# Batch 2's q and k casts and transposes moved ahead within batch 1, the output weights and batch 3's loads behind them

## Chip, cores and metric

The kernel runs on one core of one Trainium2 chip. The metric is the time of one execution on the device in microseconds (us), the median of several runs. Lower is better.

## What is computed

Sliding-window attention with a linear position bias for 8 batches of 8 heads, 576 tokens and 64 channels, and behind it a two-layer block on the 4608 x 512 result:

```
scores = q k^T / 8, for 0 <= i - j < 128, plus -slope_h * (i - j); elsewhere -1e9
attn   = softmax(scores);  x = attn v, as (4608, 512)
h      = x w_in            # w_in 512 x 2048
g      = h * clip(h + 3, 0, 6) / 6
out    = g w_out           # w_out 2048 x 512
```

Inputs and output are float32; the products run in bf16.

## The kernel before, in words

*Two streams of work on PE.* Attention is done by pairs of heads: 4 pairs per batch, so pair g belongs to batch g // 4, and there are 32 pairs. The two-layer block is done in 9 tiles of 512 tokens, cut into units: an up unit (`moe_up`, L299 on) makes 128 of the 2048 hidden channels with four 128x512 products (L303), an activation on ACT (L307) and a multiply on DVE (L308); a down unit (`moe_down`) adds four products (L320) to the output of 128 tokens. `fill(n)` puts the next n units between the steps of attention. It stops early where an up unit needs tokens of a batch whose attention isn't through.

*The order is written out by hand.* All five engines run under a manual schedule, so each engine executes its instructions in the order of the code. `first_batch` does batch 0; `segment` (L413) does the pairs 4 to 31, and in its step g: `scores(g)`, the exponentials of pair g, `values` of pair g-1 in two parts, `back(g-1)`, and then `stage_next(g)` (L359), which prepares later batches. Between these stand the fills.

*How a pair gets its q and k.* For batches 0 and 1 q and k are loaded as runs of six tokens and transposed on PE (L191). From batch 2 on, q, k and v are loaded by tokens (`load_tokens`, L105: five DMAs of 128 tokens each on SP's queue), cast by GpSimd from float32 to bf16 (`cast_tokens`, L153), and q and k are then transposed by one DMA each on SP's queue (`xbar`, L167) out of the one buffer `tbuf` into `qTb` or `kTb`. So q must have left `tbuf` before k is cast into it, and so on. v is cast into `vbuf` (L157, L160). There are four load buffers, `ldbuf`, given out by `slot_of` (L87).

*What else GpSimd does.* For every pair it applies the window mask: two selects on `pd` (L226), two on `po` (L242) and one on `p4buf` (L246), each after an exponential of ACT; `values` reads their results. It also issues the loads of the weights, which cast to bf16 on the way: `w_in` early and `w_out` (L144, four DMAs) in `load_weights_out`.

*The order around the change.* Before `segment`, SP's queue is given v of batch 1 and q and k of batch 2. Then `stage_next` puts in, always behind the selects of the pair: in pair 4, the cast of batch 1's v; in pair 5, cast and transpose of batch 2's q, then the load of batch 3's q; in pair 6, cast and transpose of batch 2's k, the load of batch 2's v, the issue of `w_out`, the load of batch 3's k; in pair 7, the cast of batch 2's v, the load of batch 3's v, the cast of batch 3's q; in pair 8, the transpose of batch 3's q and the cast of its k. In the text, q2 stands for batch 2's q, and so on.

Of the kernel before, what the change touches and what calls it, by code (L numbers as in the profile page):

```python
# [18 lines left out]
def kernel(  # L19
# [10 lines left out]
    B, H, S, D = q.shape  # L30
# [5 lines left out]
    NP = H // 2  # L36
# [50 lines left out]
    def slot_of(b, nm):  # L87
        if nm != "v" and b < 2:
            return 2 * b
        if b < 2:  # L90
            return 1 - b
        return (1, 3, 2, 0)[(3 * (b - 2) + "qkv".index(nm)) % 4]
# [6 lines left out]
    def load_runs(b, hs):  # L99
        for nm in "qk":  # L100
            nc.gpsimd.dma_start(
                out=ld[b, nm][:, hs, :],
                in_=src_of[nm][b, hs, :, :].rearrange("h (p t) d -> p h (t d)", t=RT))

    def load_tokens(b, nm):  # L105
        t = ldbuf[slot_of(b, nm)][:, 0:NQ * H * D].rearrange("p (j h d) -> p j h d", j=NQ, h=H)
        ld[b, nm] = t
        for j in range(NQ):
            n = min(128, S - j * 128)
            nc.sync.dma_start(out=t[:n, j, :, :],  # L110
                              in_=src_of[nm][b, :, ds(j * 128, n), :].rearrange("h p d -> p h d"))
# [24 lines left out]
    def load_weights_in(lo, hi):  # L136
        for g in range(lo, hi):
            nc.gpsimd.dma_start(
                out=w_in_sb[:, :, ts(g, 512)],
                in_=moe_w_in[:, ts(g, 512)].rearrange("(k p) f -> p k f", p=128))  # L140

    def load_weights_out():
        for g in range(4):
            nc.gpsimd.dma_start(  # L144
                out=w_out_sb[:, ts(g, 4), :],
                in_=moe_w_out[ds(g * 512, 512), :].rearrange("(m p) d -> p m d", p=128))
# [6 lines left out]
    def cast_tokens(b, nm):  # L153
        s = ld[b, nm]
        if nm == "v":
            for lo in (0, 2):
                nc.gpsimd.tensor_copy(  # L157
                    out=vbuf[b % 2][:, lo:lo + 2, :, 0:D].rearrange("p j h d -> p (j h) d"),
                    in_=s[:, lo:lo + 2, :, :].rearrange("p j h d -> p (j h) d"))
            nc.gpsimd.tensor_copy(out=vbuf[b % 2][:LAST, 4, :, 0:D], in_=s[:LAST, 4, :, :])  # L160
            return
        for j in range(NQ):
            m = min(128, S - j * 128)
            nc.gpsimd.tensor_copy(out=tbuf[:m, :, j, :],  # L164
                                  in_=s[:m, j, :, :].rearrange("p (i e) d -> p i (e d)", e=2))

    def xbar(b, nm):  # L167
        dst = (qTb if nm == "q" else kTb)[b % 2]
        nc.sync.dma_start_transpose(out=dst.rearrange("p h j c -> p (h j) c"),
                                    in_=tbuf.rearrange("p h j c -> p (h j c)"))  # L170
# [188 lines left out]
    def stage_next(g):  # L359
        b, hp = divmod(g, NP)  # L360
        if g == 0:
            load_runs(1, slice(0, H))
        if g == 1:
            load_weights_in(2, 4)
        if b == 1:
            if hp == 0:
                cast_tokens(1, "v")
            if hp == 1:
                cast_tokens(2, "q")
                xbar(2, "q")  # L370
            if hp == 2:
                cast_tokens(2, "k")
                xbar(2, "k")
                load_tokens(2, "v")
                load_weights_out()
            if hp == 3:
                cast_tokens(2, "v")
        if b >= 2 and b + 1 < B:
            if hp < 2:
                xbar(b + 1, "qk"[hp])  # L380
            if hp in (0, 2):
                cast_tokens(b + 1, "kkv"[hp])
        if b >= 1 and b + 2 < B:
            if hp > 0:
                load_tokens(b + 2, "qkv"[hp - 1])
            if hp == 3:
                cast_tokens(b + 2, "q")

    def first_batch():
        transposes(0)  # L390
        prepare(1)
        for g in range(NP + 1):
            if g < NP:
                scores(g)
                exp_diag(g, 0)
                exp_diag(g, 1)
            if g + 1 < NP:
                transposes(g + 1)
            if g < NP:
                exp_off(g, 0)  # L400
                exp_off(g, 1)
            if g > 0:
                values(g - 1, (0, 1, 2))
                values(g - 1, (3, 4))
            if g + 2 < NP:
                prepare(g + 2)
            if g > 0:
                back(g - 1)
                done[0] = g
            if g < NP:  # L410
                stage_next(g)

    def segment(lo, hi, fills):  # L413
        for g in range(lo, hi + 1):
# [32 lines left out]
            if g < hi:  # L447
                stage_next(g)
# [55 lines left out]
```

## Time and profile before

| | |
|---|---|
| median of 5 runs | 381.54 us (379.33 to 381.95) |
| the profiled execution's own time | 383.75 us |
| its span, first to last instruction | 382.0 us |
| PE busy | 322.5 us (84%) |
| ACT, DVE, GpSimd busy | 200.4, 172.5, 151.9 us |
| DMA | 51.64 MB, mean 135 GB/s |
| mean granted clock of PE | 0.955 |

PE is the matrix engine, ACT the scalar engine, DVE the vector engine, POOL is GpSimd and SP the engine that issues most DMAs; SPq and POOLq are instructions that issue DMAs. A row of a timeline gives the start in us from the span's start, the duration, the engine, the line of the code, the operation with what it writes and reads, and in brackets how long the engine was idle before it and what it waited for. The queue q1 carries the DMAs that SP issues, q0 those of GpSimd. The granted clock is TensorE's, as a share of full speed. A busy share of the DMA view can exceed 100%, since packets overlap.

### The profile page before, as it was taken

To read this page: it belongs to the slowest core of one execution; us is meant where nothing else is said; L and a number is where in the kernel's file an instruction comes from. 1 tells how busy PE (TensorE), PEld (TensorE's weight loads), DVE (VectorE), ACT (ScalarE), POOL (GpSimd) and SP (SyncE) were. 2 spreads that over 40 slices of the span, in tenths; PEclk is the share of its full clock that TensorE was granted. 3 is DMA by queue.
4 is the path that set the end of the run, shared out by engine and by line. 5 is a ranking of instruction groups with operands and counts; after the bars stand their busy time and mean duration, and the time that the engine had idled before them with its cause. 6 is when DMAs were issued, how large, how long until landed. Compare 5 with 4: busy or idle time off the path is not lost.

```text
span 382.0 us, 6536 instructions
## 1 busy us (share of the span) xinstructions
PE 322.5 (84%) x2445; PEld 162.3 (42%) x2445; DVE 172.5 (45%) x357; ACT 200.4 (52%) x365; POOL 151.9 (40%) x265
## 2 busy tenths in 40 slices
PE   1566877418778979988999999999999999999986
PEld 0454443213333435543555554445455444444432
DVE  5565565304535224543445454544555444344320
ACT  1643666415646346654666776657676443443401
POOL 8751385506366526735562666282334000000000
PEclk9999988856989989998999999999999999999999
DMA  9999909999979959994999699652112110010012
GB/s 170 196 208 182 203 10 185 148 208 198 200 143 218 182 129 157 221 212 118 198 211 243 141 218 222 150 116 72 47 45 47 44 53 31 27 51 33 27 57 82
DMA packets 153135, 51.64 MB, mean 135 GB/s; under 512 B 141200, under 2 KB 148624, under 8 KB 153104
## 3 DMA queue, kind: packets, MB, share of 16 engines
q1 hardware_dynamic: 145504, 44.54, 60.8%
q0 software_dynamic: 7456, 6.55, 10.8%
q8 instruction: 19, 0.31, 0.4%
q14 instruction: 12, 0.10, 0.1%
q10 hardware_dynamic: 144, 0.13, 0.1%
HBM read 36.70 MB, written 9.44 MB: 121 GB/s over the span
## 4 chain that ended last, share of the span: by engine, by line
PE 60%; ACT 8%; DVE 7%; DMA 7%; issue 6%; POOL 6%; SPq 5%; POOLq 0%
PE ops L320 27%; PE hps L303 25%; DMA xT<-avs 4%; ACT r L307 3%; SPq L110 3%; DVE g L308 2%; PE scd L203 2%; DMA ldbuf<-in_v_dram 2%; POOL tbuf L164 2%; POOL pd L226 2%; ACT pd L223 2%; PE av L266 2%; PE tp L191 2%; DMA ldbuf<-in_k_dram 1%; DVE avs L272 1%
## 5 line engine op out<-in xcount | busy, mean ns | idle before, releaser
L308 DVE SCALAR_TENSOR_TENSOR g<-r,hps 128x512 bf16<-128x512 f32 x144 | 99.0, 687 | 147.5 <-ACT r L307 147.4
L307 ACT ACTIVATE r<-hps,bias 128x512 f32<-128x512 f32 x144 | 99.6, 692 | 120.3 <-PE hps L303 119.0
L303 PE MATMUL hps<-xT,w_in_sb 128*128 128x512 bf16 x576 | 153.6, 391 | 8.6 <-DMA xT<-avs 5.6
L320 PE MATMUL ops<-w_out_sb,g 128*128 128x512 bf16 x576 | 147.5, 384 | 4.7 <-DVE osb L334 3.9
L320 PEld LDWEIGHTS <-g 128*128 128x128 bf16 x576 | 56.0, 98 | 79.6 <-issue 16.2
L303 PEld LDWEIGHTS <-w_in_sb 128*128 128x128 bf16 x576 | 53.1, 100 | 59.6 <-issue 11.0
L226 POOL TENSOR_SCALAR_AFFINE_SELECT pd<-pd 128x512 bf16<-128x512 bf16 x64 | 39.3, 633 | 64.3 <-ACT pd L223 62.6
L164 POOL CAST tbuf<-ldbuf 128x512 bf16<-128x512 f32 (+1 forms) x60 | 34.2, 615 | 36.1 <-issue 29.5
L223 ACT ACTIVATE pd<-scd,bias_d 128x512 bf16<-128x512 f32 x64 | 41.1, 684 | 13.3 <-PE scd L203 13.3
L233 ACT ACTIVATE po<-sco,bias_o 128x512 bf16<-128x512 f32 x64 | 44.3, 693 | 0.0
L242 POOL TENSOR_SCALAR_AFFINE_SELECT po<-po 128x512 bf16<-128x512 bf16 x56 | 35.4, 636 | 21.5 <-ACT po L233 19.2
L272 DVE TENSOR_TENSOR avs<-av,rc 128x384 bf16<-128x384 f32 (+1 forms) x60 | 29.7, 495 | 2.1
L263 PE MATMUL av<-vbuf,po 128*128 128x65 bf16 x240 | 24.7, 201 | 5.4 <-DVE avs L272 3.6
L266 PE MATMUL av<-vbuf,pd 128*128 128x65 bf16 x248 | 25.4, 204 | 2.0 <-POOL pd L226 2.0
L266 PEld LDWEIGHTS <-pd 128*128 128x128 bf16 x256 | 21.3, 105 | 12.6 <-POOL pd L226 3.2
L263 PEld LDWEIGHTS <-po 128*128 128x128 bf16 x256 | 21.0, 105 | 10.9 <-DVE avs L272 5.7
L203 PE MATMUL scd<-qTb,kTb 64*128 64x128 bf16 x256 | 14.4, 240 | 12.5 <-DMA kTb<-tbuf 10.8
L157 POOL CAST vbuf<-ldbuf 128x1024 bf16<-128x1024 f32 x16 | 16.3, 1040 | 17.2 <-DMA ldbuf<-in_v_dram 17.2
L271 DVE RECIPROCAL rc<-av 128x6 f32<-128x6 f32 (+1 forms) x60 | 11.0, 184 | 25.9 <-PE av L266 25.9
L236 ACT ACTIVATE p4buf<-sco,bias_d 128x64 bf16<-128x64 f32 x64 | 21.0, 328 | 0.0
L332 ACT COPY osb<-ops 128x512 f32<-128x512 f32 x18 | 10.5, 586 | 19.3 <-PE ops L320 19.3
L203 PEld LDWEIGHTS <-kTb 64*128 64x128 bf16 x256 | 8.2, 102 | 26.0 <-issue 12.1
(53 smaller groups left out, 156.4 us busy)
## 6 DMA issues: line engine op xcount, KB each, us to landing
out_dram<-osb SPq DMA_DIRECT2D x35, 256.0 KB, 2.4
ldbuf<-in_v_dram SPq DMA_DIRECT2D x32, 256.0 KB, 5.3
ldbuf<-in_q_dram SPq DMA_DIRECT2D x24, 256.0 KB, 4.7
ldbuf<-in_k_dram SPq DMA_DIRECT2D x24, 256.0 KB, 5.0
w_in_sb<-in_moe_w_in_dram POOLq DMA_DIRECT2D x4, 512.0 KB, 13.3
w_out_sb<-in_moe_w_out_dram POOLq DMA_DIRECT2D x4, 512.0 KB, 10.4
ldbuf<-in_v_dram SPq DMA_DIRECT2D x8, 128.0 KB, 5.5
ldbuf<-in_q_dram SPq DMA_DIRECT2D x6, 128.0 KB, 4.6
```

What stands on the lines that cost most here:

```text
L164: nc.gpsimd.tensor_copy(out=tbuf[:m, :, j, :], in_=s[:m, j, :, :].rearrange("p (i e) d -> p i (e d)", e=2))
L223: nc.scalar.activation(out=pd[:, e, :, :].rearrange("p j c -> p (j c)"), in_=sc[:, e, :], func=ACT.Exp, bias=bias_d[:, h:h + 1], scale=scale)
L226: nc.gpsimd.affine_select(out=pd[:, e, :, :], in_=pd[:, e, :, :], pattern=[[0, 4], [1, 128]], channel_multiplier=-1, base=0, compare_op=AL ...
L233: nc.scalar.activation(out=po[:, e, :, :].rearrange("p j c -> p (j c)"), in_=sc[:, e, :], func=ACT.Exp, bias=bias_o[:, h:h + 1], scale=scale)
L242: nc.gpsimd.affine_select(out=po[:, e, :, :], in_=po[:, e, :, :], pattern=[[0, 4], [-1, 128]], channel_multiplier=1, base=-1, compare_op=A ...
L263: nc.tensor.matmul(av[:, i, e, :], lhsT=po[:, e, qt - 1, :], rhs=vb[:, qt - 1, h, :], start=True, stop=False)
L266: nc.tensor.matmul(av[:, i, e, :], lhsT=d, rhs=vb[:, qt, h, :], start=(qt == 0), stop=True)
L272: nc.vector.tensor_tensor(out=st[g, "avs"][:, qts[0]:qts[0] + nq, :, :], in0=av[:, 0:nq, :, 0:D], in1=rc[:, 0:nq, :, :].to_broadcast([128, ...
L303: nc.tensor.matmul(hps, lhsT=w_in_sb[:, ks, ts(ms, 128)], rhs=xT[:, ks, ts(nt, NT)], start=(ks == 0), stop=(ks == n_ks - 1))
L307: nc.scalar.activation(out=r6, in_=hps, func=ACT.Relu, bias=bias3[:, 0:1], scale=1.0 / 6.0)
L308: nc.vector.scalar_tensor_tensor(out=gts[nt][:, ms, :], in0=r6, scalar=1.0, in1=hps, op0=ALU.min, op1=ALU.mult)
L320: nc.tensor.matmul(ops[nt, sub], lhsT=gts[nt][:, ms, ts(sub, 128)], rhs=w_out_sb[:, ms, :], start=(ms == 0), stop=(ms == n_ms - 1))
```

## The change

Within `stage_next`, steps move to other pairs; nothing is added or taken away. q2's cast and transpose go from pair 5 to pair 4 (behind the cast of v1), k2's from pair 6 to pair 5. The load of q3 goes from pair 5 to pair 6, behind the load of v2 and the issue of `w_out`; that of k3 from pair 6 to pair 7; that of v3 from the end of pair 7 to the start of pair 8's `stage_next`, ahead of the transpose of q3, which keeps its place. The cast of q3 stays in pair 7. From batch 2 on, the code is as before.

```diff
         if b == 1:
             if hp == 0:
                 cast_tokens(1, "v")
-            if hp == 1:
                 cast_tokens(2, "q")
                 xbar(2, "q")
-            if hp == 2:
+            if hp == 1:
                 cast_tokens(2, "k")
                 xbar(2, "k")
+            if hp == 2:
                 load_tokens(2, "v")
                 load_weights_out()
+                load_tokens(3, "q")
             if hp == 3:
                 cast_tokens(2, "v")
+                load_tokens(3, "k")
+                cast_tokens(3, "q")
+        if g == 2 * NP:
+            load_tokens(3, "v")
         if b >= 2 and b + 1 < B:
             if hp < 2:
                 xbar(b + 1, "qk"[hp])
             if hp in (0, 2):
                 cast_tokens(b + 1, "kkv"[hp])
-        if b >= 1 and b + 2 < B:
+        if b >= 2 and b + 2 < B:
             if hp > 0:
                 load_tokens(b + 2, "qkv"[hp - 1])
             if hp == 3:
```

On SP's queue the order q2's transpose, q3's load, k2's transpose, v2's load, k3's load, v3's load becomes q2's transpose, k2's transpose, v2's load, q3's load, k3's load, v3's load. On GpSimd, the casts of q2 and k2 each move ahead of the selects of one pair. The order of the operations on PE, ACT and DVE is the same in both.

## The prediction

> **What bounds the kernel now.** I read the chain of work that ended last first, then PE's waits, then the timelines of PE, SP and GpSimd from 45 to 112 us, and the DMA queues microsecond by microsecond. From 140 us on PE is busy nearly all the time. The stretch that the change touches holds PE's longest wait:
>
> ```profile
> 73.25 0.28 PE L292 MATMUL tb<-ident,avs 128*128 128x128 bf16 x2 [1.21 <-DVE avs L272]
> 84.29 0.61 PE L203 MATMUL scd<-qTb,kTb 64*128 64x128 bf16 x8 [10.76 <-DMA kTb<-tbuf]
> 95.67 0.20 PE L266 MATMUL av<-vbuf,pd 128*128 128x65 bf16 x1 [0.23 <-POOL pd L226]
> 107.64 0.20 PE L266 MATMUL av<-vbuf,pd 128*128 128x65 bf16 x1 [0.99 <-POOL pd L226]
> ```
>
> Columns: start, duration, instruction, and in brackets the idle time before it with its releaser. Pair 8 (the first of batch 2) waits 10.76 us for batch 2's k. The next two rows are pairs 8 and 9 entering `values`, each held by GpSimd. Why GpSimd is late there stands in its own timeline:
>
> ```profile
> 47.30 2.02 POOL L157 CAST vbuf<-ldbuf 128x1024 bf16<-128x1024 f32 x2
> 54.16 3.08 POOL L164 CAST tbuf<-ldbuf 128x512 bf16<-128x512 f32 x5
> 64.04 2.83 POOL L164 CAST tbuf<-ldbuf 128x512 bf16<-128x512 f32 x5
> 66.82 2.99 POOL L144 DMA_DIRECT2D w_out_sb<-in_moe_w_out_dram  x4
> 86.79 1.04 POOL L157 CAST vbuf<-ldbuf 128x1024 bf16<-128x1024 f32 x1 [13.35 <-DMA ldbuf<-in_v_dram]
> 92.19 2.84 POOL L164 CAST tbuf<-ldbuf 128x512 bf16<-128x512 f32 x5
> 104.16 2.83 POOL L164 CAST tbuf<-ldbuf 128x512 bf16<-128x512 f32 x5 [6.54 <-DMA qTb<-tbuf]
> ```
>
> In order: casts of v1, q2, k2, the four w_out issues, casts of v2, q3, k3. Pair 9's selects are queued behind the cast of k3, which waits until q3's transpose has emptied `tbuf`. That transpose is the last of a long row on SP:
>
> ```profile
> 57.27 3.19 SPq L169 DMA_TRANSPOSE qTb<-tbuf  x1
> 60.51 4.44 SPq L110 DMA_DIRECT2D ldbuf<-in_q_dram  x5
> 66.90 9.53 SPq L169 DMA_TRANSPOSE kTb<-tbuf  x1
> 76.54 9.69 SPq L110 DMA_DIRECT2D ldbuf<-in_v_dram  x5
> 86.28 6.57 SPq L110 DMA_DIRECT2D ldbuf<-in_k_dram  x5
> 92.90 5.63 SPq L110 DMA_DIRECT2D ldbuf<-in_v_dram  x5
> 98.69 3.83 SPq L169 DMA_TRANSPOSE qTb<-tbuf  x1
> ```
>
> What the DMA engines did in one microsecond, 76 to 77 (w_out in flight) and 86 to 87 (w_out done); columns: packets, MB, share:
>
> ```profile
> q0 software_dynamic: 166, 0.15, 90.9%
> q1 hardware_dynamic: 164, 0.04, 30.5%
> ...
> q1 hardware_dynamic: 857, 0.22, 137.4%
> ```
>
> While w_out runs, SP's queue gets a fifth of the bytes: 0.04 MB per us against 0.22. So k2's transpose took 17.3 us to land where q2's took 5.1, and it is the DMA engines that are short from 57 to 104 us, not SP's time.
>
> **What the Trainium skill says.** (1) "DMA: Bandwidth & Descriptors", Queues, rings and completion order: each engine goes round-robin between queue rows packet by packet. The trace agrees: 166 packets against 164; the bytes differ because w_out's packets hold about four times as much. (2) The same page, Issuing engines are not separate DMA queues: issuing from another engine adds no bandwidth. The trace agrees: 0.15 + 0.04 is no more than 0.22. (3) "Perfetto Trace Analysis", Summary: the profiler window per engine type: a DMA instruction's duration doesn't contain the movement of its data. The trace agrees (q2's transpose: 3.19 us of issue, 5.1 to landing), so I take arrivals from the time to landing in the issue view. (4) "TensorE: Matmul & The Clock Gate", Part 1: the clock halves after idling and returns after some 3.4 us of work. The trace agrees on the half: the granted clock is 0.50 from 84.3 to 91.1 and 0.66 from 107.6 to 112.
>
> **The change, part by part.**
>
> *q2's cast moves from pair 5 to pair 4.* The v1 cast ends at 49.9 (49.27 + 0.61); five casts take 2.83, so q2 is cast at 52.7 instead of 57.2. Its transpose goes out on SP at 52.7; the DMA engines are empty from 48.2 to 58, so it lands 5.1 later, at 57.8. Pair 5's first select, at 50.24 before, now starts at 52.7 and its group of five (2 x 0.63, 2 x 0.63, 0.29, about 2.7) ends at 55.4 instead of 54.2. Pair 5's `values` starts at 59.45, so this is hidden with 4 us to spare.
>
> *k2's cast moves from pair 6 to pair 5.* It must wait for q2's transpose, because `tbuf` is single: 57.8 to 60.7. Behind it on GpSimd stand pair 6's selects (first at 60.12 before, now 60.7), and they catch up, since the last ones wait for ACT until 63.2 anyway; wanted at 68.84. Cost nothing. k2's transpose is issued at 60.75 and lands at 65.9, if w_out doesn't reach it. PE wants it at 73.5: the 10.76 us stall goes.
>
> *w_out.* Without a cast ahead of it, its issue comes after pair 6's selects, at 64.04 instead of 66.82. First packets came 1.4 us after issue before, so about 65.5: k2's transpose is nearly through. It moves 2.1 MB at 0.155, 13.5 us: before, it ended at 83.0; now at 79.0, or 80.2 if the slow start of before (20 and 70 packets in its first two microseconds) is repeated. Its first use is pair 9's first down product (102.37 before): covered by over 15 us.
>
> *The loads.* SP now issues v2 (from 63.9), then q3, k3, v3, then q3's transpose. What the change takes from w_out's shadow is k2's transpose (128 x 2560 x 2 B = 0.655 MB); what it puts in is v2 and q3, 1.18 MB each. q3 had run at full rate at 60.5 to 67.2.
>
> **What is late next.** By w_out's end SP's queue has moved 13 x 0.04 + 0.05 = 0.57 MB of v2. v2 needs 0.61 more (2.9 us) and q3 5.5: q3 lands at about 88.5 instead of 68.4 (63.8 + 4.6). The cast of q3 ends at 89.2 (it follows the landings chunk by chunk, one 0.6 cast behind the last), pair 8's selects 2.4 later, so pair 8's first `values` ends at 91.8 against 97.8: six of the ten microseconds survive to this point, and PE has waited idle from 84.7 to 89.8.
>
> The second gate takes most of those. q3's transpose is behind v2, q3, k3, v3: 4 x 1.18 + 0.655 = 5.375 MB, less 0.57, leaves 4.8 MB. Before, from 83.0 to 103.8, the queue moved the rest of k2's transpose (0.13), v2, k3, v3 and that transpose, 4.33 MB in 20.5 us: 0.211 MB per us. So now 22.7 us, from 79.0 or 80.2: landing at 102.0 or 103.2 against 103.8 to 104.1. Put as a ledger of the engines: before they stood nearly empty only from 67.2 to 69.9; now the wait for `tbuf` empties them from 57.5 to 61.7. The earlier start is mostly spent there. I take the middle, 102.6: 1.5 us earlier. Cast k3 (2.83) and a select (0.63) follow as before, so pair 9's `values` starts at 106.1 instead of 107.64.
>
> PE isn't the later one: from 91.8 it has the 9.0 us of work that lay between 97.6 and 106.6, and about 2 us for the half clock after its idling, so it is ready at 102.8 and idles 3.3 us. Half clock afterwards exists in both (0.66 from 107.6 to 112), so I cost it at nothing; bounds: 1 us better if the window falls well, 1.5 us worse after the longer idling. From there the order on all engines is the same and follows PE.
>
> Sum: from 73.5, PE comes to pair 8's `values` at 84.7 (95.4 - 84.3 = 11.2 of work, half of it at half clock as before) and waits there till 89.8: 5.1. So -10.76 + 5.1 + 3.3 (wait before pair 9) + about 0.8 (more half clock between the two) = -1.5 us. Against the profiled execution: 383.75 (span 382.0) becomes 382.2. That one lies 2.2 above the median of the five runs, 381.54; the same difference gives 380.0.
>
> **Rivals.**
>
> *The gates are lighter than I think* (0.20): no slow start, the loads at 0.22 throughout, and no dip like the one at 90 us (0.10 MB). Then 4.75/0.22 = 21.6 from 79.0: 100.6, or 3.4 earlier, where PE's own readiness (102.8) nearly takes over. 378.1, at best 376.8. For it: most full microseconds show 0.21 to 0.22.
>
> *The stall's whole worth stays* (0.05): if pair 9's selects didn't wait on the DMA queue, 381.5 - 10 = 371. The 6.54 us wait for q3's transpose speaks against.
>
> *w_out overtakes k2's transpose* (0.12), the slower ending. It decides at GpSimd's and SP's order around 61 to 65 us: if k2's transpose gets going only when w_out's packets come (in before, both issued at 66.9, it got 15 packets in the first 3 us), it crawls at 0.04 until 79.6, leaving 5.4 MB behind w_out; 25.6 us more puts q3's transpose at 105.5, 1.5 later than before, and 1 to 1.5 us of half clock comes on top: 384.3. Against: 3.3 us of lead, when q2's whole transpose needs 5.1.
>
> *Nothing arrives* (0.08): the slow start and the dip both repeat, and the landing is at 103.8: 381.5.
>
> **How the numbers follow.** Forecast 0.55, its own range 379.2 to 381.0. Half a per cent, about what a measurement of this kernel can tell from no change, is 1.9 us: below 379.6 counts as faster, above 383.4 as slower. Of the forecast 0.17 lies below 379.6, 0.38 within. Faster: 0.17 + 0.20 + 0.05 = 0.42; same 0.38 + 0.08 = 0.46; slower 0.12. The range 377.0 to 382.6 leaves out the whole-stall case, the slower one and a little of the first rival: 0.2.
>
> **What would show it.** Right: no wait of PE for k2 at pair 8; w_out issued near 64; a new PE wait of some 6 us ahead of pair 8's `values`, released by GpSimd, whose q3 cast waits for q3's load; GpSimd's k3 cast starting near 102.6 to 103. Wrong: q3 landing before 84, or k3's cast starting before 100 (gain of 3 us or more), or PE still waiting for k2 at 73.5.

## The result, and the profile after

The changed kernel takes 385.04 us (median of 37 runs) against 380.95 before (median of 72). The ratio is 1.0101, with a 95% interval of 1.0082 to 1.012: about 3.9 us slower. The ratio leaves out runs more than 1.5% above the fastest of their kernel, so it is a little smaller than that of the two medians. The forecast was 380.0, with a range up to 382.6. The profiled execution after has a span of 383.2 us and its own time is 384.91.

PE's timeline after, at the places shown before (start, duration, instruction, idle time before it and its releaser):

```profile
73.11 0.40 PE L203 MATMUL scd<-qTb,kTb 64*128 64x128 bf16 x8
...
93.03 0.23 PE L266 MATMUL av<-vbuf,pd 128*128 128x65 bf16 x1 [8.95 <-POOL pd L226]
...
109.68 0.23 PE L266 MATMUL av<-vbuf,pd 128*128 128x65 bf16 x1 [4.54 <-POOL pd L226]
```

Pair 8's scores start at 73.11 without a wait: the 10.76 us for k2 are gone. In their place pair 8 waits 8.95 us (0.23 before) and pair 9 waits 4.54 us (0.99 before) for GpSimd's selects. Pair 8 enters `values` 2.6 us earlier than before, pair 9 2.0 us later. GpSimd's timeline shows what its selects stood behind:

```profile
49.42 2.84 POOL L164 CAST tbuf<-ldbuf 128x512 bf16<-128x512 f32 x5
59.09 2.84 POOL L164 CAST tbuf<-ldbuf 128x512 bf16<-128x512 f32 x5 [4.12 <-issue]
64.48 2.99 POOL L144 DMA_DIRECT2D w_out_sb<-in_moe_w_out_dram  x4
82.77 1.04 POOL L157 CAST vbuf<-ldbuf 128x1024 bf16<-128x1024 f32 x1 [9.68 <-DMA ldbuf<-in_v_dram]
91.78 0.61 POOL L164 CAST tbuf<-ldbuf 64x512 bf16<-64x512 f32 x1 [0.20 <-DMA ldbuf<-in_q_dram]
106.20 2.84 POOL L164 CAST tbuf<-ldbuf 128x512 bf16<-128x512 f32 x5 [11.21 <-DMA qTb<-tbuf]
```

These are the casts of q2 and k2, the issue of w_out, the first cast of v2, the last of q3's five, and k3's. q3's last chunk is cast at 91.8 to 92.4; the cast of k3 waits 11.21 us until q3's transpose has landed at 106.1 (99.37 + 6.7 from issue to landing). For the 4.12 us before k2's cast the profile names no releaser; the cast starts 0.1 us after q2's transpose has landed (52.29 + 6.7). SP's queue in the same stretch:

```profile
52.29 3.18 SPq L169 DMA_TRANSPOSE qTb<-tbuf  x1
61.96 3.01 SPq L169 DMA_TRANSPOSE kTb<-tbuf  x1
65.09 17.35 SPq L110 DMA_DIRECT2D ldbuf<-in_v_dram  x5
82.49 5.54 SPq L110 DMA_DIRECT2D ldbuf<-in_q_dram  x5
88.07 5.45 SPq L110 DMA_DIRECT2D ldbuf<-in_k_dram  x5
93.56 5.64 SPq L110 DMA_DIRECT2D ldbuf<-in_v_dram  x5
99.37 3.81 SPq L169 DMA_TRANSPOSE qTb<-tbuf  x1
```

Before, the issues held up in w_out's company were k2's transpose (9.53 us) and then v2's load (9.69). Now v2's load alone is held up for 17.35 us, with q3, k3 and v3 behind it. In the microsecond from 76 to 77 the DMA view after has nearly the same shares as before:

```profile
q0 software_dynamic: 154, 0.16, 92.4%
q1 hardware_dynamic: 152, 0.04, 29.4%
```

From 57.1 to 63 the DMA engines stood empty, two packets apart.

### The profile page after: what moved, and what is told of

Its sections match the earlier page's. It is cut to its first block, busy times and chain, and to the rows that moved or that the text cites. A ratio compares the mean times of both kernels' runs of the same rounds, so it can differ in the third digit from the quotient of the medians.

```text
span 383.2 us, 6538 instructions
## 1 busy us (share of the span) xinstructions
PE 324.3 (85%) x2445; PEld 162.2 (42%) x2445; DVE 174.1 (45%) x357; ACT 200.9 (52%) x365; POOL 152.6 (40%) x265
## 4 chain that ended last, share of the span: by engine, by line
PE 56%; SPq 11%; DVE 8%; ACT 8%; issue 6%; DMA 6%; POOL 4%; POOLq 0%
PE ops L320 25%; PE hps L303 23%; SPq L110 10%; ACT r L307 3%; DMA xT<-avs 3%; DVE g L308 2%; ACT pd L223 2%; PE scd L203 2%; DMA qTb<-tbuf 2%; POOL pd L226 2%; DVE avs L272 2%; DMA ldbuf<-in_q_dram 2%; PE av L266 1%; ACT po L233 1%; PE tp L191 1%
## 5 line engine op out<-in xcount | busy, mean ns | idle before, releaser
L303 PE MATMUL hps<-xT,w_in_sb 128*128 128x512 bf16 x576 | 156.4, 397 | 7.2 <-DMA xT<-avs 4.5
L226 POOL TENSOR_SCALAR_AFFINE_SELECT pd<-pd 128x512 bf16<-128x512 bf16 x64 | 39.6, 640 | 61.7 <-ACT pd L223 60.7
L191 PE MATMUL tp<-ident,pr 96*128 96x96 bf16 x96 | 8.9, 265 | 10.6 <-DVE pr L179 9.0
L292 PE MATMUL tb<-ident,avs 128*128 128x128 bf16 x45 | 6.9, 267 | 11.0 <-DVE avs L272 10.8
```

Of the source, the lines that this page charges most:

```text
L226: nc.gpsimd.affine_select(out=pd[:, e, :, :], in_=pd[:, e, :, :], pattern=[[0, 4], [1, 128]], channel_multiplier=-1, base=0, compare_op=AL ...
L303: nc.tensor.matmul(hps, lhsT=w_in_sb[:, ks, ts(ms, 128)], rhs=xT[:, ks, ts(nt, NT)], start=(ks == 0), stop=(ks == n_ks - 1))
```

## The experiments

Theory G, the one of the prediction, now with other sizes: GpSimd works in order, so whatever its casts wait for delays the selects behind them; they wait for the row of DMAs on SP's queue, and the row is long because it lies in w_out's shadow. Theory C: the loss is the half clock after PE's two long waits. Theory R: the early casts and transposes cost the time themselves. Theory O: the loss is outside this stretch.

The table has the times. Each ratio is to runs of the kernel before that were taken beside it, so the ratio is the fair figure. The last two columns come from PE's timeline: the time from the first scores of pair 7 to those of pair 11, which holds all that the change touches, and from there to pair 31.

| kernel | median us | ratio to before (interval) | pair 7 to 11 | 11 to 31 |
|---|---|---|---|---|
| before | 380.95 | | 51.56 | 172.43 |
| before_again | 380.06 | 0.9994 (0.9964 to 1.0025) | 51.56 | 169.11 |
| after | 385.04 | 1.0101 (1.0082 to 1.012) | 54.15 | 171.19 |
| after_again | 385.28 | 1.0148 (1.0092 to 1.0203) | 54.87 | 171.15 |
| v3_behind | 376.96 | 0.9919 (0.9894 to 0.9945) | 45.79 | 170.98 |
| two_tbuf | 380.94 | 1.0019 (0.9993 to 1.0044) | 49.35 | 171.47 |
| q3_early | 375.86 | 0.9864 (0.9805 to 0.9923) | 47.14 | 169.11 |
| loads_only | 388.80 | 1.0222 (1.0165 to 1.028) | 59.84 | 169.24 |
| q3_early_v3 | 373.81 | 0.9831 (0.9783 to 0.988) | 45.38 | 170.72 |
| wout_hole | 375.63 | 0.987 (0.9825 to 0.9916) | 45.35 | 170.09 |
| wout_pair7a | 373.30 | 0.9826 (0.9787 to 0.9864) | 43.79 | 169.69 |
| wout_pair7b | 373.88 | 0.9849 (0.9803 to 0.9895) | 44.51 | 169.58 |
| k3_late | 382.21 | 1.0059 (1.0032 to 1.0085) | 45.90 | 176.85 |
| best | 370.51 | 0.974 (0.9697 to 0.9782) | 33.49 | 178.39 |

### The two kernels once more: before_again and after_again

No edit.

> The kernel before once more, for a second profile: the profiled execution before (383.75) lies 2.8 us above the median of its runs (380.95), the one after (384.91) at its median. Theory G (the row of DMAs ahead of q3's transpose sets pair 9's start): pair 9 enters values within 0.5 us of 107.64 again, and executions differ only later, in PE's waits for the transposes of the result. Rival O (the loss is outside the stretch from 60 to 112 us): the two profiles of before differ already at pair 9 by 2 us or more. Time: ratio 1.000 within 0.3%.

> The changed kernel once more, for a second profile. Theory G: q3's transpose lands at 106 within 0.5 us, pair 9 enters values at 109.7, as in the first profile, so 2 us of the loss are this gate in every execution. Rival O: pair 9's start moves by 2 us or more between executions, and the first profile showed only one of several cases. Time: 1.010 of before within 0.3%.

The stretch is 51.56 us in both profiles before and 54.15 and 54.87 after, so 2.6 to 3.3 us of the 3.9 are lost there in each execution, and theory O falls for the main part. In before_again pair 9 stands at 109.50 instead of 107.64, against the expectation, but only because everything from pair 2 on is 1.8 us later (pair 2's scores at 23.72 instead of 21.90). In after_again it stands at 110.97, another 1.3 us later than after, since q3's transpose landed at 107.3 and not, as expected, within 0.5 us of 106. Behind pair 11 the two profiles before differ by 3.3 us, more than either differs from after; so the rest of the 3.9 us can't be placed from four profiles.

### v3's load behind q3's transpose: v3_behind

```diff
-        if g == 2 * NP:
-            load_tokens(3, "v")
...
                 xbar(b + 1, "qk"[hp])
+                if g == 2 * NP:
+                    load_tokens(3, "v")
```

> The changed kernel, but v3's load is issued behind q3's transpose instead of ahead of it. Theory G: 1.18 MB at 0.21 MB per us, 5.6 us, leave the row ahead of the transpose; it lands at about 100.4 instead of 106.05, the cast of k3 ends at 103.3, PE's wait of 4.54 us before pair 9 goes to nothing, and the kernel is about 4.5 us faster than the changed one: 380.5, about the time before (-0.5 to +0.3%). Rival C (the loss is half clock after the two long waits): only the second of the two idlings goes, so at most 1.5 us come back: 383.5. Rival O: no change, 385.

It is 8.3 us below after_again, measured beside it, and 0.8% below the kernel before. The transpose is issued 6 us earlier, as G says, and it lands at 98.5 (93.22 + 5.3); k3's cast and pair 9's `values` follow:

```profile
93.22 3.79 SPq L169 DMA_TRANSPOSE qTb<-tbuf  x1
97.06 4.75 SPq L110 DMA_DIRECT2D ldbuf<-in_v_dram  x5
...
98.62 2.83 POOL L164 CAST tbuf<-ldbuf 128x512 bf16<-128x512 f32 x5 [4.01 <-DMA qTb<-tbuf]
...
104.83 0.23 PE L266 MATMUL av<-vbuf,pd 128*128 128x65 bf16 x2
```

PE has no wait before pair 9, while pair 8's wait is there as it was (8.39 us). I had expected 4.5 us; 8.3 came. The wait of 4.54 was little more than half of what that gate costs. The changed kernel's PE timeline shows the rest:

```profile
110.27 0.23 PE L266 MATMUL av<-vbuf,pd 128*128 128x65 bf16 x1 [0.35 <-POOL pd L226]
110.85 0.24 PE L263 MATMUL av<-vbuf,po 128*128 128x65 bf16 x1 [0.35 <-POOL po L242]
...
111.44 0.24 PE L263 MATMUL av<-vbuf,po 128*128 128x65 bf16 x1 [0.30 <-POOL po L242]
...
111.76 1.90 PE L320 MATMUL ops<-w_out_sb,g 128*128 128x512 bf16 x4
113.45 1.90 PE L303 MATMUL hps<-xT,w_in_sb 128*128 128x512 bf16 x4
```

Ten products that take 0.3 us back to back last from 109.68 to 111.76, since each of four selects has to come first (1.8 us), and the two units after them run at 1.90 instead of 1.03 (starts 1.7 apart instead of 0.86: some 1.7 us). 4.5 + 1.8 + 1.7 = 8.0; from pair 10's scores to pair 11's v3_behind is 8.1 us shorter (8.46 against 16.52). Theory C has a part in it, as a follower of the wait, not as a cause.

### A second buffer for k2: two_tbuf

```diff
+    tbuf2 = ldbuf[0][:, :].bitcast(BF16)[:, 0:NP * NQ * 128].rearrange(
+        "p (h j c) -> p h j c", h=NP, j=NQ)
+
+    def tbuf_of(b, nm):
+        return tbuf2 if (b, nm) == (2, "k") else tbuf
```

`cast_tokens` and `xbar` use it in the place of `tbuf`, and DVE clears its last rows.

> The changed kernel, but k2 is cast into a second buffer (the load buffer that v1 has left), so its cast needn't wait until q2's transpose has emptied the first. Theory G with the hole as its cause: the cast starts at 55.0 instead of 59.09, the transpose of k2 is issued at 57.8 instead of 61.96, v2's load gets 4 us at full rate ahead of w_out (0.85 MB), q3's transpose lands 4 us earlier (102), pair 9 starts 4 us earlier (105.7): 381, about the time before. If the hole is not the cause (w_out or the slow end of q3's own transpose is), the landing stays at 105 or later and the time at 384 to 385.

380.94, 4.3 us below after_again, as expected; but the hole is only shortened. The cast of k2 starts at 55.3 and ends at 58.2, and its transpose goes out at 59.76:

```profile
59.35 0.27 DVE L170 MEMSET ldbuf<- 64x256 uint32 x1
59.76 3.02 SPq L178 DMA_TRANSPOSE kTb<-ldbuf  x1
```

What it waited for, by the profile, is DVE's clearing of the second buffer's last rows, which this edit brings in; q2's transpose landed at about the same time (52.81 + 6.7), so the trace can't tell whether that would have held it too. The changed kernel does issue the transpose of pair 8's result at 103.28 with q3's still in flight, so a transpose doesn't always wait for the one before it. The engines stood nearly empty for 3.4 us instead of 6, and q3's transpose lands at 103.1, 2.9 us earlier than in the changed kernel, not 4.

### Which part did it: q3_early and loads_only

q3_early leaves q3's load behind q2's transpose:

```diff
                 xbar(2, "q")
+                load_tokens(3, "q")
...
                 load_weights_out()
-                load_tokens(3, "q")
```

> The changed kernel, but q3's load stays right behind q2's transpose (in pair 4), so only the transposes, k3 and v3 are moved. Theory G (the row of DMAs behind w_out): q3's 1.18 MB fill the stretch from 57 to 62 us in which the DMA engines stood empty, and leave the row. Pair 8 then waits for v2 alone and enters values at about 91 (93.0 in the changed kernel); q3's transpose lands at about 99 instead of 106, so pair 9 waits no more than 1 us. 375, some 10 us below the changed kernel. Rival R (the early casts and transposes themselves cost the time): they are as early here, so 384 to 385.

loads_only is the opposite half, against the changed kernel:

```diff
-                cast_tokens(2, "q")
-                xbar(2, "q")
             if hp == 1:
+                cast_tokens(2, "q")
+                xbar(2, "q")
+            if hp == 2:
                 cast_tokens(2, "k")
                 xbar(2, "k")
-            if hp == 2:
                 load_tokens(2, "v")
```

> The kernel before with only the loads moved as in the change (q3 behind v2 and w_out, k3 and v3 after it); the casts and transposes of q2 and k2 stay in pairs 5 and 6. Theory G: PE waits for k2 some 10 us before pair 8 as before, and q3's 1.18 MB are added to the row behind w_out: q3's transpose lands 5.6 us later than before (109.6), pair 9 enters values at about 113, 387 (1.5% over before). Rival R: without the early transposes no loss, 380 to 381.

They settle it. With the transposes early and q3's load where it was: 375.86, 1.4% faster than before. With the loads moved alone: 388.80, 2.2% slower. So the transposes' move is a gain and theory R falls; what loses is that q3's load was put behind w_out (k3's and v3's loads stay in their order behind v2's in both). The two add up: -1.4% and +2.2% make +0.8%, and the whole change has +1.0%. In q3_early q3's load fills the empty stretch, and the row is shorter by it (SP's timeline):

```profile
55.70 5.25 SPq L110 DMA_DIRECT2D ldbuf<-in_q_dram  x5
62.13 3.17 SPq L169 DMA_TRANSPOSE kTb<-tbuf  x1
65.42 17.91 SPq L110 DMA_DIRECT2D ldbuf<-in_v_dram  x5
...
94.06 3.78 SPq L169 DMA_TRANSPOSE qTb<-tbuf  x1
```

Pair 8 still waits 6.30 us, for v2 alone. In loads_only PE waits for k2 again, and then for the selects behind q3's cast (and 4.50 us once more before pair 9):

```profile
83.28 0.61 PE L203 MATMUL scd<-qTb,kTb 64*128 64x128 bf16 x8 [10.38 <-DMA kTb<-tbuf]
...
98.09 0.23 PE L266 MATMUL av<-vbuf,pd 128*128 128x65 bf16 x1 [3.67 <-POOL pd L226]
```

### The two cures together: q3_early_v3

Both edits above.

> q3's load early and v3's load behind q3's transpose. Theory G: the two edits take away the same wait before pair 9, so they don't add up; pair 8's wait for v2 is left. 374 to 375.5, no more than 1 us below q3_early. If the two gains add up (5 us or more below q3_early), pair 9's gate isn't what either removed.

373.81, 2 us below q3_early and so a little better than foreseen, but far from the sum (8.3 and 9.4 us below the changed kernel each). They act on the same gate: q3_early has no wait left before pair 9, but its selects still feed the ten products one by one, with the half clock behind them (11.97 us from pair 10's scores to pair 11's); with v3 behind too this is 8.46. Pair 8's wait, 9.39 us in this profile, is left.

### Where to put w_out: wout_hole, wout_pair7a, wout_pair7b

wout_hole issues w_out in pair 4, behind q2's transpose, with k2's cast and transpose in pair 6 and v3's load behind q3's transpose:

```diff
                 xbar(2, "q")
-            if hp == 1:
+                load_weights_out()
+            if hp == 2:
                 cast_tokens(2, "k")
                 xbar(2, "k")
-            if hp == 2:
                 load_tokens(2, "v")
-                load_weights_out()
```

> w_out is issued in pair 4 behind q2's cast and transpose, where the DMA engines stand empty from 48 us on; k2's cast and transpose are in pair 6 as before the change, v3's load behind q3's transpose. Theory G: w_out runs from 54 to 67 with nothing but q2's transpose beside it; k2's transpose lands at about 72, in time for pair 8 at 73.3; v2, q3 and k3 then come at full rate (77, 83, 88), so pair 8 waits no more than 1 us instead of 9 and pair 9 not at all: 366 to 369. If DMA were not what the stretch is short of, it would stay near the 377 of v3_behind.

That missed: 375.63. The expectation had forgotten its own rule. q2's transpose, now w_out's companion, took 18.0 us to land; k2's cast needs the buffer that it holds, and PE waited for k2:

```profile
70.02 2.83 POOL L164 CAST tbuf<-ldbuf 128x512 bf16<-128x512 f32 x5 [6.68 <-issue]
```

```profile
77.86 0.61 PE L203 MATMUL scd<-qTb,kTb 64*128 64x128 bf16 x8 [5.04 <-DMA kTb<-tbuf]
...
91.77 0.24 PE L266 MATMUL av<-vbuf,pd 128*128 128x65 bf16 x1 [2.83 <-POOL pd L226]
```

The other two start from q3_early_v3 and issue w_out in pair 7, ahead of v2's cast (a) or behind q3's (b):

```diff
-                load_weights_out()
             if hp == 3:
+                load_weights_out()
                 cast_tokens(2, "v")
```

> As q3_early_v3, but w_out is issued a pair later, in pair 7 ahead of v2's cast (GpSimd at about 73 instead of 64). Theory G: v2 comes at full rate (landed by 73 instead of 86), so pair 8 waits no more than 1 us instead of 6 to 9; k3 and q3's transpose are now in w_out's shadow (75 to 89), so q3's transpose lands near 94 and pair 9 waits 2 to 4 us. 367 to 371, 3 to 7 below q3_early_v3 (373.8). If pair 8's wait isn't v2 behind w_out, 373 to 375.

> As wout_pair7a, but w_out is issued behind the casts of v2 and q3, at about 79 on GpSimd, so that k3's load has passed and q3's transpose starts together with it. Theory G: pair 8 doesn't wait; q3's transpose, in the shadow from its start, lands at w_out's end near 94, and pair 9 waits as in wout_pair7a or 1 to 2 us longer; w_out's last part is wanted at about 95 and lands by then. 367 to 371. If w_out is late for the first down product of pair 9, PE shows a wait for w_out there.

Half right: pair 8 doesn't wait in either, so its wait was v2 behind w_out. But pair 9's came back, 5.99 and 6.75 us, twice what I gave it, and the times, 373.30 and 373.88, are those of q3_early_v3. In wout_pair7a GpSimd stands 12.39 us ahead of k3's cast:

```profile
95.98 2.83 POOL L164 CAST tbuf<-ldbuf 128x512 bf16<-128x512 f32 x5 [12.39 <-DMA qTb<-tbuf]
```

In each of the three places the transfer that was wanted next and ran beside w_out became the new wait: q2's transpose and so k2, then twice q3's.

### Taking the cast out of the selects' way: k3_late and best

Every DMA keeps its place; only k3's cast goes behind pair 9's selects:

```diff
+            if g == 2 * NP + 1:
+                cast_tokens(3, "k")
             if hp < 2:
                 xbar(b + 1, "qk"[hp])
...
-            if hp in (0, 2):
+            if hp in (0, 2) and g != 2 * NP:
                 cast_tokens(b + 1, "kkv"[hp])
```

> The changed kernel, but the cast of k3 is issued in pair 9, behind pair 9's selects, instead of in pair 8 ahead of them; every DMA keeps its place in the row. Theory G says that the row costs time only because the cast of k3, which waits for q3's transpose, stands on GpSimd ahead of pair 9's selects: q3's transpose lands at 105 to 106 as in the changed kernel, PE's wait of 4.54 us before pair 9 goes, 376 to 378 as with v3_behind. Rival: if the DMA row holds PE in another way (k3, v3 or the transposes themselves), 381 to 385.

> wout_pair7a with the cast of k3 in pair 9 too. wout_pair7a moved pair 8's wait to pair 9 (5.99 us, GpSimd waiting 12.4 us for q3's transpose in w_out's shadow). Theory G: without that queueing PE waits at neither pair: 6.0 of wait, about 1 between the selects and 1 to 2 of half clock go, 364 to 366. If the wait comes back at pair 10 (whose selects then stand behind the cast of k3), 368 to 373.

Up to pair 11 theory G holds: in k3_late q3's transpose lands as late as in the changed kernel (k3's cast at 106.22), PE doesn't wait before pair 9, and the stretch is 45.90 us, as in v3_behind. But the time is 382.21, not 376 to 378, and lies in the rival's range: the late row holds PE in another way too. The wait moved to pair 13's result:

```profile
130.12 0.38 PE L303 MATMUL hps<-xT,w_in_sb 128*128 128x512 bf16 x1 [2.03 <-DMA xT<-avs]
137.35 0.59 PE L303 MATMUL hps<-xT,w_in_sb 128*128 128x512 bf16 x1 [6.86 <-DMA xT<-avs]
```

The transposes of the result (`back`, L285) are on SP too, in order behind the loads. Batch 4's loads are behind k3's transpose, which is late, and so the result's transpose of 128.40 in v3_behind comes at 133.17. PE, no longer held at pair 9, runs into it: 2.03 + 6.86 us, where v3_behind waits 3.33. So the cast ahead of the selects is only the first place where the row's lateness reaches PE. best, which is wout_pair7a with this edit, gains 10 us up to pair 11 and gives some 9 back behind it (178.39 against 169.69; 6.86 us of it is a wait at the same place, 3.03 one behind an ACT copy). At 370.51, not the 364 to 366 of theory G, it is still the fastest of all: 2.6% below the kernel before (0.9697 to 0.9782).

## Why the prediction was wrong

The chain of causes was right, link by link, and a size in it was wrong. The profiled execution was to take 382.2 and took 384.91, 2.7 us more; the median was to be 380.0 and is 385.04. The further 2.3 us come from the assumption that the profiled execution lies 2.2 us above its median again; this time it lies on it. The failing term is the arrival of q3's transpose: "landing at 102.0 or 103.2 ... I take the middle, 102.6: 1.5 us earlier". It landed at 106.1, 2 us later than before, and pair 9's `values` started at 109.68 instead of the forecast 106.1.

- *k2's stall goes.* Right: no wait at 73.11, and k2's transpose landed 4.9 us after its issue. The rival in which w_out overtakes it had nearly the measured time (384.3), but didn't happen.
- *q2's transpose lands 5.1 after issue.* It took 6.7 (6.5 to 6.9 in every run that had it in pair 4 without w_out behind it). The empty stretch became 6 us instead of 4.2, the first of three small overruns. In two_tbuf, shortening it by 2.6 us went with 4.3 us of time.
- *w_out ends at 79.0 or 80.2.* It ended at 81.5: issued 0.44 later, behind the late cast of k2, with a slow start like that of before (30 and 54 packets in its first two microseconds) and 0.14 MB per us for four more. That is 1.9 us over the middle.
- *4.8 MB at 0.211 take 22.7 us.* They took 24.5, from 81.5 to 106: 0.196 MB per us, the last transpose alone 6.7 instead of 5.2. Another 1.5 to 1.8. The rate itself was read a little too high: from 83.0 to 103.8 is 20.8 us, not 20.5, so 4.33 MB make 0.208, which is 0.3 to 0.4 us of it.
- *Pair 8 waits 5.1 us.* 8.95, since q3 came 3.2 us later than 89.2. The expected line of the profile was there, with the releaser named.
- *Pair 9 waits 3.3 us, and half clock costs nothing more.* 4.54 us. The price that I left out is what v3_behind shows: such a wait also stretches the products behind it and halves the clock, 8 us for a visible wait of 4.5. Most of this belonged to the kernel before as well (0.99 us of wait, the same slow group, 1.90 and 1.54 for the two units), so the difference was small; but it means that every microsecond at this gate was worth keeping, and that the gate, not the stall at pair 8, was the thing to ask about. The 3.4 us of work that the prediction cites for the clock's return were 6.8 us in its own trace (half clock from 84.3 to 91.1, with PE busy for 5.5 of them).
- *The range.* It was built from a sum whose three terms all had a bad end (the landing of a lone transpose, the slow start, the row's rate), and I let the ends cancel. With w_out's end and the row's time as measured, 81.5 + 24.5, the same arithmetic gives 106; since the 24.5 is read from that landing, this only says where the miss sits.

What the prediction didn't see at all is that the change is two changes of opposite sign. It had written down both ("q3 had run at full rate at 60.5 to 67.2"; "now the wait for `tbuf` empties them from 57.5 to 61.7"), and never priced them apart. The runs do: transposes early -1.4%, q3's load behind w_out +2.2%, each done alone.

The two transposes that took 6.7 us have something in common. In the last microseconds of each, the DMA view has one packet of a third queue, which it calls "instruction" (after, 56 to 57 and 104 to 105):

```profile
q1 hardware_dynamic: 583, 0.14, 80.5%
q8 instruction: 1, 0.02, 5.8%
...
q1 hardware_dynamic: 541, 0.13, 118.2%
q8 instruction: 1, 0.02, 6.0%
```

Before, that packet came at 55, with nothing in flight, and at 104.5, when q3's transpose had landed. In the fourteen profiles, 15 transposes of q2 or q3 clear of w_out have such a packet some 4 to 5 us after their issue, and they landed after 6.5 to 7.1 us; the 25 of q2, k2, q3 or k3 clear of w_out that have none landed after 4.9 to 5.3; three that have it earlier, after 5.4 to 6.1. So about 1.5 us of each of the two landings goes with where this packet fell, and the prediction had nothing for it. No run moved the packet by itself, so that it is the cause is argued, not shown.

Open: about 1 us of the 3.9, which four profiles can't place. Buffers for two transposes at a time were tried only in the one place.

## What to carry to other kernels

Draw up the row of transfers behind a big one, with who waits for the last of them and what stands behind that waiter on its engine; then price each moved transfer by whether it runs in the shadow or in a hole, one by one. A stall that is removed ahead of an in-order queue can show up at the queue's end: look for the next thing that the same row delivers. And count a wait with what follows it: the slow group and the half clock here nearly doubled it (4.5 us became 8).

## What the runs showed of the hardware

- A GpSimd-issued load of 1 KB packets beside SP's 256-byte packets left SP about 0.04 of 0.20 MB per us in every run, wherever it was put (mostly 140 to 170 packets per us on each queue once it was under way). The Trainium skill's round robin by packets ("DMA: Bandwidth & Descriptors", Queues, rings and completion order) is seen here at its price: a transpose issued together with the load lands after 17 to 18 us, where 5 are enough alone.
- A transpose of 0.655 MB clear of w_out landed after 4.9 to 5.3 us (25 of them), but after 6.5 to 7.1 when one packet of the queue "instruction" came some 4 to 5 us after its issue (15 of them).
- Two profiles of one kernel can differ by 3.3 us in a stretch that nothing has touched (172.43 and 169.11 from pair 11 to 31).
